# A decode block with an 8192-row KV cache: bias columns inside the first load, and the first load in 16 and 112 rows

## The chip, the cores and the metric

The kernel runs on one core of one Trainium2 chip. The metric is device time in microseconds (us) of one execution. Three executions of the kernel before took 1050.42, 1050.46 and 1050.50 us; the median is 1050.46 us. A profile of one more execution, of 1050.38 us, is what all views are taken from.

## The reference

One token goes through an attention block with a cached key and value store, and then through a dense block; both are modulated by a vector `c`. All data are float32. B_b1 and B_b2 are the two biases of the dense block; they are what the change handles differently.

```python
mod = (silu(c) @ w_mod).reshape(1, 6, 1, 640)          # sa, ca, ga, sb, cb, gb
h = layernorm(x) * (1 + ca) + sa
q = (h @ wq).reshape(32 heads, 192)
p = softmax(q . k_cache / sqrt(192))                   # 32 heads, 8192 keys each
o = p . v_cache                                        # 32 x 192
x = x + ga * (o @ wo)
h = layernorm(x) * (1 + cb) + sb
h = relu(h @ w1 + B_b1) ** 2                           # 640 -> 1536
x = x + gb * (h @ w2 + B_b2)                           # 1536 -> 640
```

The two caches are 32 x 8192 x 192 floats each, 403 MB together; the weights make up the rest of the 451.82 MB that the page of the profile counts as read.

## The kernel before

**Loads.** All loads go through one queue, issued by SyncE (SP in the profile) in the order of the program. The SBUF holds three large buffers, `slot`, of 128 rows, and every large load takes the next of the three in turn: first the load `first` (the modulation weights of two of the six parts, the query weights of the first pair of heads, and the columns of `c` and `x`, 8330 floats a row), then the keys of head 0, the values of head 0, the keys of head 1, and so on, `load_k(h)` and `load_v(h)`. Beside the keys, most rows of `in_kx` carry a piece of the weights `wq` or `wo` that a later step needs. Behind the last head come the weights of the dense block. A load into a slot waits until the work that read the slot's old content is done. So the keys of head 1 wait until all that reads `first` is done, the values of head 1 wait for the work on the keys of head 0, and the keys of head 2 for the work on the values of head 0. In this text k0 and v0 are the loads of keys and values of head 0, k1 and v1 those of head 1, and so on.

**Start.** Before head 0 can be worked on, the vector `silu(c)` is made (an exponential on ScalarE, ACT in the profile, then VectorE, DVE), the modulation of the first layer norm is weighed and summed (`weigh`, DVE and TensorE, PE), the layer norm is put together, and `query(0, ...)` multiplies its result with the query weights that lie in the slot of `first` (lines 352 to 381). Then `spread(x_c, KB, "x_t")` (line 382) copies the five columns of `x` on ACT to a tile `spread`, of which there is one buffer, each column 32 times side by side, and DVE transposes that to the tile `x_t`. This is the last read of the slot of `first`.

**A head.** `keys` multiplies the keys with the query in place (DVE, the group `slot<-slot,qb`), adds halves (GpSimd, POOL) and reduces (DVE, `sc`); `softmax` finds the maximum (DVE `mp`, PE transpose, DVE `nm`) and takes the exponential (ACT `p`); `values` multiplies with the values on PE. From head 1 on, `own` and `turn` bring the output of the head before into form.

**Biases.** The tile `bbc` holds 12 columns of B_b1 and 5 of B_b2. It is loaded after `load_v(0)` by four loads, of 8, 4, 12 and 104 rows of 17 floats (`BB_CUT`, lines 484 to 488). At head 3, before its `keys`, `spread(bbc, FB + KB, "bbt")` (line 490) brings them through the same tile `spread` to `bbt`, 544 floats a row. `bbt` is first read behind the last head, at lines 569 and 581.

**Waits.** A helper class records every operation and works out which semaphores it has to wait for; that is why nearly every row of the profile bears line 167. Each load counts on one of eight semaphores, `load0` to `load7`, in turn. Where an operation waits for several semaphores, the helper writes a wait for each, in front of the operation (lines 159 to 163):

```python
for w in waits:
    if w == "token":
        engine.wait_ge(sems[w], 1).then_inc(sems[w], -1)
    else:
        engine.wait_ge(sems[w[0]], w[1])
```

When the program is built, the last of these waits goes into the operation itself, and the others stay as instructions of their own ahead of it. The loads of ACT's function tables (`ACT_TABLE_LOAD`) are put in by the build, directly ahead of the operation that needs the table.

Of the kernel before, what the change touches and what calls it, by code (L numbers as in the profile page):

```python
# [11 lines left out]
P = 128  # L12
D = 640
# [7 lines left out]
KB = DG // 32  # L21
FB = FG // 32
# [5 lines left out]
WQ = KB * PW  # L28
ROW = KV + WO
WM = KB * 2 * D  # L30
VEC = 2 * KB
DA = 128
DB = DH - DA
REP = 8
# [2 lines left out]
WO_AT = {2 * i + 4: i for i in range(-1, NPAIR - 2)} | {H - 1: NPAIR - 2}  # L37
WQ_AT = {2 * i + 1: i + 1 for i in range(NPAIR - 1)}
WIDE = {h for h, i in (WO_AT | WQ_AT).items() if i >= 0}
BB_CUT = (8, 4, 12, 104)  # L40
HALF = DG // 2
W2_CUT = (0, 6 * D, 9 * D, 11 * D, 11 * D + G * HALF, FB * D)
EPS = 1e-5
# [180 lines left out]
    return b[1] <= a[1] and a[2] <= b[2] and b[3] <= a[3] and a[4] <= b[4]  # L224


def block_kernel(nc, first, kx, vx, wm1, w1, w2, bb, out):
    def const(shape, name):
        return nc.tile(shape, name)

    def work(shape, tag, bufs=2):
        return nc.tile(shape, tag, bufs)
# [6 lines left out]
    def slot():  # L239
        return nc.tile([P, ROW], "slot", 3, align=512)  # L240

    k_t, v_t = {}, {}
    first_t = slot()
    nc.sync.dma_start(first_t[:, :WM + WQ + VEC], first)

    ident = const([P, P], "ident")
    make_identity(nc, ident)
# [12 lines left out]
                            axis=AX.X, op=ALU.add)  # L260
# [3 lines left out]
                            axis=AX.X, op=ALU.add)  # L264
# [5 lines left out]

    vec = first_t[:, WM + WQ:WM + WQ + VEC]
    c_c = vec[:, :KB]
    x_c = vec[:, KB:2 * KB]
    bbc = const([P, FB + KB], "bbc")

    def load_k(h):
        k_t[h] = slot()
        n = K_PARTS.get(h, 1)
        cuts = [KV * c // n for c in range(n)] + [ROW if h in WIDE else KV]
        for a, b in zip(cuts, cuts[1:]):  # L280
            nc.sync.dma_start(k_t[h][:, a:b], kx[h, :, a:b])

    def load_v(h):
        v_t[h] = slot()
        nc.sync.dma_start(v_t[h][:, :KV], vx[h])
# [7 lines left out]
    def spread(src, n, name):  # L293

        t = work([P, FB + KB, 32], "spread", 1)
        nc.scalar.copy(t[:, :n], src[:, :, None].to_broadcast([P, n, 32]))
        r = const([P, 32 * n], name)
        nc.vector.transpose(r, t[:, :n].rearrange("p b r -> p (b r)"))
        return r

    def total(src, name):

        ps = psum("sm")
        n = src.shape[1]
        nc.tensor.matmul(ps[:, :n], ones, src, start=True, stop=True)
        return ps[:, :n]
# [35 lines left out]
    def attend(i, w, oT):  # L342

        nc.fresh = True
        for j in range(3):
            for g in range(G):
                nc.tensor.matmul(att[32 * g:32 * (g + 1), :DG], oT[:, j:j + 1].to_broadcast([P, 32]),
                                 w[:, j, DG * g:DG * (g + 1)], start=False, stop=(i == NPAIR - 1 and j == 2))
# [24 lines left out]
    def query(i, w):  # L373
        w = w.rearrange("p (b n) -> p b n", b=KB)
        ps = psum("q", at=0)
        for b in range(KB):
            nc.tensor.matmul(ps[:, :PW], h1[:, b:b + 1].to_broadcast([P, P]), w[:, b], start=(b == 0), stop=(b == KB - 1))
        qb_t[i] = work([P, PW], "qb")
        nc.scalar.activation(qb_t[i], ps[:, :PW], AF.Copy, scale=DH ** -0.5)

    query(0, first_t[:, WM:WM + WQ])
    x_t = spread(x_c, KB, "x_t")

    ri_t, o_t, sp_t, os_t, sum_t, m_t, pt_t = {}, {}, {}, {}, {}, {}, {}

    def keys(h, between):

        q = qb_t[h // 2][:, DH * (h % 2):DH * (h % 2 + 1)]
        sc = work([P, NPOS], "sc")
        t = k_t[h][:, :KV].rearrange("p (i d) -> p i d", d=DH)  # L390
        sums = SUMS.get(h, ((32, 0),))
        n = NPOS // len(sums)
        for c, (nf, na) in enumerate(sums):
            a, b = n - nf - na, n - na
            pr = t[:, c * n:(c + 1) * n]
            s = sc[:, c * n:(c + 1) * n]
            nc.vector.tensor_mul(pr, pr, q[:, None, :].to_broadcast([P, n, DH]))
            nc.gpsimd.tensor_add(pr[:, a:b, :DH // 2], pr[:, a:b, :DH // 2], pr[:, a:b, DH // 2:])
            for i in range(b, n):
                jk = work([P, DH], "jk")  # L400
                nc.scalar.activation(jk, pr[:, i], AF.Copy, accum_out=s[:, i:i + 1])
            nc.vector.tensor_reduce(s[:, :a], pr[:, :a], axis=AX.X, op=ALU.add)
            if c == 0:
                between()
            nc.vector.tensor_reduce(s[:, a:b], pr[:, a:b, :DH // 2], axis=AX.X, op=ALU.add)
        return sc

    def softmax(h, sc):
        mp = work([P, 1], "mp")
        nc.vector.tensor_reduce(mp, sc, axis=AX.X, op=ALU.max)  # L410
        ps = psum("sm")
        nc.tensor.transpose(ps[:, :P], mp.to_broadcast([P, P]), ident)
        nm = work([P, 1], "nm")
        nc.vector.tensor_reduce(nm, ps[:, :P], axis=AX.X, op=ALU.max, negate=True)

        p = work([P, NPOS, REP], "p", 1)
        i = h // 2
        if h % 2 == 0:
            sp_t[i] = work([P, 2], "sp", 3)
        nc.scalar.activation(p, sc[:, :, None].to_broadcast([P, NPOS, REP]), AF.Exp, bias=nm,  # L420
                             accum_out=sp_t[i][:, h % 2:h % 2 + 1])
        return p
# [17 lines left out]
    def own(h, after=None):  # L440

        i, a = h // 2, h % 2
        if not a:
            m_t[i] = work([P, 2, 1024], "own", 1)
            os_t[i] = work([P, P], "os", 3).rearrange("p (a d) -> p a d", a=2)
        if i not in ri_t and (a or i == NPAIR - 1):
            ri_t[i] = work([P, 2], "ri", 3)
            nc.vector.reciprocal(ri_t[i], sum_t.pop(i))
        m, o = m_t[i][:, a], o_t.pop(h)
        cuts = (0, 512, 1024) if h == H - 1 else (0, 1024)  # L450
        for lo, hi in zip(cuts, cuts[1:]):
            nc.vector.tensor_mul(m[:, lo:hi], o[:, lo:hi], mask[:, lo:hi], after=after)
        if i == NPAIR - 1:
            nc.vector.tensor_reduce(os_t[i][:, a], m[:, 512:].rearrange("p (j d) -> p d j", d=DB), axis=AX.X, op=ALU.add)
        elif a:
            nc.vector.tensor_reduce(os_t[i], m_t[i][:, :, 512:].rearrange("p a (j d) -> p a d j", d=DB), axis=AX.X, op=ALU.add)

    def turn(i, heads=(0, 1)):

        if i not in pt_t:  # L460
            pt_t[i] = psum("sm")
        pt = pt_t[i]
        for a in heads:
            nc.tensor.matmul(pt[DB * a:DB * (a + 1), 2:3], os_t[i][:, a], ri_t[i][:, a:a + 1], start=True, stop=True)
        for a in heads:
            for j in range(4):
                nc.tensor.matmul(pt[:, a:a + 1], m_t[i][:, a, DA * j:DA * (j + 1)], ri_t[i][:, a:a + 1],
                                 start=(j == 0), stop=(j == 3))
        if 1 in heads:
            oT_t[i] = work([P, 3], "oT", 3)  # L470
            nc.scalar.copy(oT_t[i], pt[:, :3])
# [4 lines left out]
    for h in range(H):  # L476
        i = h // 2
        if h % TURN == 1 and (h < H - 1 or nc.turns):
            nc.loop(h < H - 1)
        if h:  # L480
            load_k(h)
        load_v(h)
        if h == 0:
            nc.gpsimd.memset(v_t[0][:, KV:ROW], 0.0)
            r0 = 0
            for n in BB_CUT:
                nc.sync.dma_start(bbc[r0:r0 + n], bb[r0:r0 + n])
                r0 += n
        if h == 3:
            bbt = spread(bbc, FB + KB, "bbt")  # L490

        def wo():
            if h in WO_AT:
                attend(WO_AT[h], k_t[h][:, KV:ROW].rearrange("p (j n) -> p j n", j=3), oT_t.pop(WO_AT[h]))

        def between():
            if h in WQ_AT:
                query(WQ_AT[h], k_t[h][:, KV:ROW])
            if h < H - 1:
                wo()  # L500

        sc = keys(h, between)
        p = softmax(h, sc)
        if h == H - 1:
            sum_t[i] = total(sp_t.pop(i), f"sum{i}")
            wo()
        if h:
            own(h - 1, qb_t.get(h // 2 + 1))
        if h % 2 == 0 and h:
            turn(i - 1)  # L510
        if h == H - 1:
            turn(i, (0,))
        values(h, p)
        if h % 2 and h < H - 1:
            sum_t[i] = total(sp_t.pop(i), f"sum{i}")
# [132 lines left out]
```

## Time and profile before

| what | value |
|---|---|
| median of three runs | 1050.46 us (1050.42 to 1050.50) |
| time of the profiled execution | 1050.38 us |
| its span, first to last instruction | 1049.1 us |
| read from memory | 451.82 MB |
| instructions | 6398 |

Time and span differ by 1.3 us, which lie before the first and after the last instruction. In the views, times are microseconds from the start of the span. A row of the timeline reads: start, duration, engine (SPq is the queue of SyncE, PEld a weight load of PE), line, operation, destination<-sources, shape, count, and in brackets how long the engine had been idle and what ended that. A row of the windows reads: the stretch, its length, busy time of the five engines with their instruction counts, the granted TensorE clock, the share of the 16 DMA engines and the rate in GB/s. Packets are put into the window in which they start, whole, so in a short window share and rate can be far above what the engines can carry; they then tell how many packets started there.

### The profile page before, as it was taken

How to read it: one execution, taken by the hardware profiler on the slowest of the kernel's cores; microseconds unless marked ns; L12 is line 12 of the kernel's file. 1: busy time of each engine (PE TensorE's matmuls, PEld its weight loads, DVE VectorE, ACT ScalarE, POOL GpSimd, SP SyncE). 2: the span in 40 equal slices, each digit the busy share in tenths (PEclk: the TensorE clock that was granted, in tenths of full speed). 3: DMA queues.
4: the chain of work that ended last, by engine and by line, in shares of the span. 5: the costliest groups of instructions: out<-in, count | busy, mean ns of one | idle time of the engine just before them, and what ended most of it. 6: DMA issues, size and time to landing. Idle time of an engine off the chain costs nothing. (4 is left out here: it accounts for less than half of the span.)

```text
span 1049.1 us, 6398 instructions
## 1 busy us (share of the span) xinstructions
PE 457.0 (44%) x2736; PEld 207.5 (20%) x2736; DVE 829.3 (79%) x284; ACT 69.0 (7%) x247; POOL 213.3 (20%) x50
## 2 busy tenths in 40 slices
PE   1153452535445064453526355163443516353456
PEld 0011221112122031222203122121212103121223
DVE  6788778988787987878888787897878798778852
ACT  1000000000000000000000000000000000012330
POOL 1221122221122221022222022222012222022100
PEclk9666665766657576675666658566665766666569
DMA  9999999999999999999999999999999999999998
GB/s 403 446 429 430 419 448 433 422 448 431 430 427 437 445 424 440 435 435 429 428 446 431 431 426 444 437 427 437 437 430 427 435 444 433 428 440 435 428 424 357
DMA packets 11266, 451.99 MB, mean 431 GB/s; under 512 B 1525, under 2 KB 1781, under 8 KB 2037
## 3 DMA queue, kind: packets, MB, share of 16 engines
q1 hardware_dynamic: 11253, 451.83, 99.6%
q8 instruction: 7, 0.11, 0.0%
q14 instruction: 6, 0.05, 0.0%
HBM read 451.82 MB, written 0.00 MB: 431 GB/s over the span
## 5 line engine op out<-in xcount | busy, mean ns | idle before, releaser
L167 DVE TENSOR_TENSOR slot<-slot,qb 128x12288 f32<-128x12288 f32 (+2 forms) x37 | 415.3, 11225 | 133.3 <-DMA slot<-in_kx 133.3
L167 POOL TENSOR_TENSOR slot<-slot 128x3072 f32<-128x3072 f32 (+2 forms) x37 | 210.3, 5683 | 791.6 <-DVE slot L167 791.6
L167 DVE TENSOR_REDUCE sc<-slot 128x32 f32<-128x6144 f32 (+5 forms) x74 | 307.0, 4150 | 13.3 <-POOL slot L167 12.0
L167 PE MATMUL ps_o<-slot,p 128*32 128x512 f32 x1536 | 240.8, 791 | 22.2 <-PEq L161 21.0
L167 PE MATMUL ps_q<-slot,ln_h 128*128 128x384 f32 x160 | 88.9, 728 | 80.6 <-PEq L161 79.3
L167 PE MATMUL ps_sm<-ident,mp 128*128 128x128 f32 x32 | 14.0, 438 | 248.9 <-PEq L161 213.0
L167 PEld LDWEIGHTS ps_o<-slot,p 128*32 128x32 f32 x1536 | 63.4, 140 | 175.3 <-issue 171.6
L167 PE MATMUL ps_q<-slot,oT 128*32 128x160 f32 x408 | 29.5, 453 | 154.6 <-PEq L161 154.4
L167 PEld LDWEIGHTS ps_q<-slot,ln_h 128*128 128x128 f32 x160 | 45.4, 296 | 128.5 <-issue 122.7
L167 PEld LDWEIGHTS ps_sm<-ident,mp 128*128 128x128 f32 x32 | 5.7, 179 | 267.3 <-issue 229.9
L167 ACT ACTIVATE p<-sc,nm 128x512 f32<-128x512 f32 x32 | 23.1, 721 | 525.7 <-DVE nm L167 525.7
L167 PE MATMUL ps_sm<-ri,own 128*128 128x1 f32 x256 | 56.5, 350 | 0.0
L167 PEld LDWEIGHTS ps_sm<-ri,own 128*128 128x128 f32 x256 | 55.0, 326 | 0.2
L167 PEld LDWEIGHTS ps_q<-slot,oT 128*32 128x32 f32 x408 | 18.2, 158 | 158.1 <-issue 155.2
L167 DVE TENSOR_TENSOR own<-ps_o,mask 128x1024 f32<-128x1024 f32 (+1 forms) x33 | 38.9, 1178 | 9.5 <-PE ps_o L167 9.5
L167 DVE TENSOR_REDUCE os<-own 128x128 f32<-128x1024 f32 (+1 forms) x17 | 30.2, 1774 | 0.6
L167 PE MATMUL ps_sm<-ri,os 128*64 128x1 f32 x64 | 6.4, 247 | 55.1 <-POOLq L165 54.4
L167 DVE TENSOR_REDUCE nm<-ps_sm 128x1 f32<-128x128 f32 x32 | 9.3, 292 | 21.2 <-PE ps_sm L167 21.2
L167 ACT ACTIVATE jk<-slot 128x192 f32<-128x192 f32 x69 | 24.0, 349 | 32.0 <-DVE slot L167 32.0
L167 ACT ACTIVATE qb<-ps_q 128x384 f32<-128x384 f32 x16 | 7.8, 490 | 272.8 <-PE ps_q L167 272.8
L167 PEld LDWEIGHTS ps_sm<-ri,os 128*64 128x64 f32 x64 | 5.3, 203 | 60.4 <-issue 58.4
L167 ACT ACTIVATION_READ_ACCUMULATOR jk<-slot 128x1 f32 x69 | 12.9, 187 | 0.0
(81 smaller groups left out, 93.4 us busy)
## 6 DMA issues: line engine op xcount, KB each, us to landing
slot<-in_kx SPq DMA_DIRECT2D x28, 7104.0 KB, 28.1
slot<-in_vx SPq DMA_DIRECT2D x32, 6144.0 KB, 22.6
slot<-in_kx SPq DMA_DIRECT2D x2, 6144.0 KB, 25.4
slot<-in_kx SPq DMA_DIRECT2D x2, 4032.0 KB, 23.8
slot<-in_kx SPq DMA_DIRECT2D x2, 3072.0 KB, 16.9
slot<-in_first SPq DMA_DIRECT2D x1, 4165.0 KB, 12.5
slot<-in_wm SPq DMA_DIRECT2D x1, 3840.0 KB, 25.5
slot<-in_w SPq DMA_DIRECT2D x1, 3840.0 KB, 31.8
```

Source lines behind the costliest of these rows:

```text
L167: i = getattr(engine, name)(*args, **kwargs)
```

## The change

The 17 bias columns become part of the rows of `first`: the host appends them, so that a row has 8347 floats, and `bbc` is now a view of the slot. The four bias loads and `BB_CUT` go. `first` is loaded by two loads, rows 0 to 15 and rows 16 to 127, instead of one. `spread(bbc, FB + KB, "bbt")` moves from head 3 to directly behind the one of `x_t`, because the slot is overwritten by k1.

```diff
-VEC = 2 * KB
+VEC = 3 * KB + FB
-BB_CUT = (8, 4, 12, 104)
...
     first_t = slot()
-    nc.sync.dma_start(first_t[:, :WM + WQ + VEC], first)
+    for a, b in ((0, 16), (16, P)):
+        nc.sync.dma_start(first_t[a:b, :WM + WQ + VEC], first[a:b])
...
-    bbc = const([P, FB + KB], "bbc")
+    bbc = vec[:, 2 * KB:]
...
     query(0, first_t[:, WM:WM + WQ])
     x_t = spread(x_c, KB, "x_t")
+    bbt = spread(bbc, FB + KB, "bbt")
...
         if h == 0:
             nc.gpsimd.memset(v_t[0][:, KV:ROW], 0.0)
-            r0 = 0
-            for n in BB_CUT:
-                nc.sync.dma_start(bbc[r0:r0 + n], bb[r0:r0 + n])
-                r0 += n
-        if h == 3:
-            bbt = spread(bbc, FB + KB, "bbt")
...
-        "first": np.concatenate([rows(wm[:, :2 * D], KB), wq[0], column(c, KB), column(a(A_x).ravel()[order], KB)], axis=1),
+        "first": np.concatenate([rows(wm[:, :2 * D], KB), wq[0], column(c, KB), column(a(A_x).ravel()[order], KB),
+                                 column(B_b1, FB), column(a(B_b2)[order], KB)], axis=1),
```

Two places show what the built programs have in another order. The first is ACT at the start, up to the exponential of the first head. In brackets stand the semaphores that are waited for ahead of a row or by it; `load0` and `load1` are those of the first and the second load of the program. Before:

```order
L167 ACT_TABLE_LOAD [waits barrier_Pool_Activation_PE_DVE_SP_release]
L167 ACTIVATE silu<-slot 128x5 [waits load0]
L167 ACT_TABLE_LOAD
L167 ACTIVATE ln_sd<-ps_sm,eps_t 128x1 [waits tensor]
L167 ACTIVATE qb<-ps_q 128x384 [waits tensor]
L167 COPY spread<-slot 128x160
L167 ACT_TABLE_LOAD
L167 ACTIVATE p,sp<-sc,nm 128x512 [waits vector]
```

The same place of ACT in the changed program:

```order
L166 ACT_TABLE_LOAD [waits barrier_Pool_Activation_PE_DVE_SP_release,load1]
L166 ACTIVATE silu<-slot 128x5 [waits load0]
L166 ACT_TABLE_LOAD
L166 ACTIVATE ln_sd<-ps_sm,eps_t 128x1 [waits tensor]
L166 ACTIVATE qb<-ps_q 128x384 [waits tensor]
L166 COPY spread<-slot 128x160
L166 COPY spread<-slot 128x544 [waits vector]
L166 ACT_TABLE_LOAD
L166 ACTIVATE p,sp<-sc,nm 128x512 [waits vector]
```

Two things moved: the exponential now depends on two loads, and the wait for the second of them (`load1`, the 112 rows) stands ahead of the first table load; and the copy of the bias columns stands behind the copy for `x_t`, with a wait for DVE.

The second place is DVE around the first head, from the transpose to `x_t` to the multiplication of the second head's keys. Before:

```order
L167 STREAM_TRANSPOSE x_t<-spread 128x160 [waits scalar]
L167 TENSOR_TENSOR slot<-slot,qb 128x12288 [waits load1]
L167 TENSOR_REDUCE sc<-slot 128x32 [waits vector]
L167 TENSOR_REDUCE sc<-slot 128x32 [waits gpsimd]
L167 TENSOR_REDUCE mp<-sc 128x1 [waits vector]
L167 TENSOR_REDUCE nm<-ps_sm 128x1 [waits tensor]
L167 TENSOR_TENSOR slot<-slot,qb 128x12288 [waits load7]
```

The same place of DVE in the changed program:

```order
L166 STREAM_TRANSPOSE x_t<-spread 128x160 [waits scalar]
L166 STREAM_TRANSPOSE bbt<-spread 128x544 [waits scalar]
L166 TENSOR_TENSOR slot<-slot,qb 128x12288 [waits load2]
L166 TENSOR_REDUCE sc<-slot 128x32 [waits vector]
L166 TENSOR_REDUCE sc<-slot 128x32 [waits gpsimd]
L166 TENSOR_REDUCE mp<-sc 128x1 [waits vector]
L166 TENSOR_REDUCE nm<-ps_sm 128x1 [waits tensor]
L166 TENSOR_TENSOR slot<-slot,qb 128x12288 [waits load4]
```

The transpose to `bbt` now stands ahead of the first large multiplication; before, it stood ahead of that of head 3.

More of the change, by code (lines that the diff above doesn't have):

```diff
@@ L224, in within, with block_kernel @@
     return b[1] <= a[1] and a[2] <= b[2] and b[3] <= a[3] and a[4] <= b[4]
-def block_kernel(nc, first, kx, vx, wm1, w1, w2, bb, out):
+def block_kernel(nc, first, kx, vx, wm1, w1, w2, out):
     def const(shape, name):
@@ L637 @@
         "w2": w2,
-        "bb": np.concatenate([column(B_b1, FB), column(a(B_b2)[order], KB)], axis=1),
     }
```

## The prediction

> **What bounds the kernel now.** I read the page of the profile first, then the chain that ended last, then windows over the whole span. The page says how full the memory path is.
>
> ```profile
> span 1049.1 us, 6398 instructions
> PE 457.0 (44%) x2736; PEld 207.5 (20%) x2736; DVE 829.3 (79%) x284; ACT 69.0 (7%) x247; POOL 213.3 (20%) x50
> q1 hardware_dynamic: 11253, 451.83, 99.6%
> ...
> 1.50:5.00 3.50, 0.00 (x0) 0.00 (x0) 2.92 (x1) 0.51 (x1) 2.31 (x7) 1.00 1.00 343
> 102.00:1020.00 918.00, 406.46 (x2311) 184.94 (x2306) 742.44 (x227) 60.54 (x230) 196.02 (x35) 0.64 1.00 433
> ...
> 1020.41 25.14 DMA slot<-in_w
> 1045.55 0.04 issue
> 1045.59 1.17 PE ps_q L167 x32
> ```
>
> The reader is to see that the packets of queue q1 fill 99.6% of the span of 16 DMA engines, that the share is 1.00 at 433 GB/s in the long middle, and that the chain ends in the last weights (`in_w`) with two microseconds of work behind them. DVE, the busiest engine, has 79%. So the time is the start of the stream of loads, plus 452 MB at the rate of the middle, plus a short end, plus every stretch in which the stream has no load to work on. The end is not edited. The change can act by an earlier or later start of the stream, by bytes and packets, and by a gap. The queue has a gap when SP issues a load too late, and SP issues a load when its slot is free. So I looked for how early each load is issued. These rows are from the timeline (the queue of SP and what holds it at the start) and from the lists of DMA issues (number, KB, time from issue to landing).
>
> ```profile
> 0.73 1.28 ACT L167 ACT_TABLE_LOAD   x1 [0.73 <-PEq L640]
> 0.74 0.38 SPq L167 DMA_DIRECT2D slot<-in_first  x1
> 1.18 0.42 SPq L167 DMA_DIRECT2D slot<-in_kx  x1
> 2.11 1.77 SPq L167 DMA_DIRECT2D bbc<-in_bb  x4
> 13.30 0.21 ACT L167 ACTIVATE silu<-slot 128x5 f32<-128x5 f32 x1 [11.29 <-DMA slot<-in_first]
> 30.90 0.32 ACT L167 COPY spread<-slot 128x160 f32<-128x160 f32 x1
> 31.24 0.36 SPq L167 DMA_DIRECT2D slot<-in_kx  x1
> 31.25 0.35 DVE L167 STREAM_TRANSPOSE x_t<-spread 128x160 f32<-128x160 f32 x1 [6.82 <-ACT spread L167]
> 31.51 12.92 DVE L167 TENSOR_TENSOR slot<-slot,qb 128x12288 f32<-128x12288 f32 x1
> 54.61 0.35 SPq L167 DMA_DIRECT2D slot<-in_vx  x1
> 59.11 12.96 DVE L167 TENSOR_TENSOR slot<-slot,qb 128x12288 f32<-128x12288 f32 x1 [3.42 <-DMA slot<-in_kx]
> ...
> slot<-in_first SPq DMA_DIRECT2D x1, 4165.0 KB, 12.5
> slot<-in_kx SPq DMA_DIRECT2D x1, 7104.0 KB, 27.9
> slot<-in_vx SPq DMA_DIRECT2D x1, 6144.0 KB, 18.9
> ...
> slot<-in_kx SPq DMA_DIRECT2D x1, 6144.0 KB, 24.2
> slot<-in_vx SPq DMA_DIRECT2D x1, 6144.0 KB, 21.8
> ```
>
> The five rows of issues are, in order, `first` (0.74), k1 (31.24), v1 (54.61), k2 and v2 (both issued between 63 and 83). `first` is the only large load that met an empty queue. Its 4165 KB are 4.27 MB, 9.8 us at 433 GB/s; it took 12.5. So a load on an empty queue costs 2.7 us beside its bytes. What another load takes beyond its bytes and these 2.7 us is time that it stood in line, and by so much it could be issued later without a gap:
>
> - k1: 7.27 MB are 16.8 us; 27.9 - 16.8 - 2.7 = 8.4 us.
> - v1: 6.29 MB are 14.5 us; 18.9 - 14.5 - 2.7 = **1.7 us**.
> - k2: 24.2 - 14.5 - 2.7 = 7.0 us. v2: 21.8 - 14.5 - 2.7 = 4.6 us.
>
> The load of the values of head 1 has the least slack at the start, 1.7 us, and it waits for DVE to be done with head 0, which in turn hangs on the prologue. A second look at the same place: packets that start around the change from k1 to v1.
>
> ```profile
> 1.70:2.00 0.30, 0.00 (x0) 0.00 (x0) 0.00 (x0) 0.30 (x1) 0.24 (x2) 1.00 5.27 1333
> 2.60:2.75 0.15, 0.00 (x0) 0.00 (x0) 0.15 (x1) 0.00 (x0) 0.15 (x1) 1.00 2.36 889
> 41.25:42.05 0.80, 0.00 (x0) 0.00 (x0) 0.80 (x1) 0.00 (x0) 0.00 (x0) 0.50 2.78 1148
> 57.90:58.15 0.25, 0.25 (x4) 0.00 (x0) 0.00 (x0) 0.00 (x0) 0.00 (x0) 0.50 0.00 0
> 58.15:58.80 0.65, 0.65 (x8) 0.20 (x4) 0.00 (x0) 0.00 (x0) 0.00 (x0) 0.50 2.81 1210
> ```
>
> All 16 engines begin v1 between 58.15 and 58.80: 1210 GB/s over 0.65 us are 0.79 MB, sixteen rows of 49 KB. At the very start 1333 GB/s over 0.30 us are twelve rows of 33 KB from 1.70 on, and four follow after 2.60. Issue was at 0.74, so a packet starts about 1.0 us after its issue, on four engines 1.9 us. For v1, issued at 54.61, that is 55.6 on most engines and 56.5 on four: 2.5 us, or 1.6 us, ahead of 58.15, when the first engine comes free. The two ways to see the slack, 1.7 us and about 2.5 us, differ by the slower first packets of a cold queue.
>
> **The change, part by part.**
>
> *Bytes.* The 8.7 KB of biases are loaded either way: 0.
>
> *Four small loads out of the queue.* SP spent 1.77 us on them at 2.11 and had nothing to issue until 31.24, so nobody gains that. Their packets lie between v0 and k1: there the sixteen engines change loads within 0.80 us (1148 GB/s are sixteen rows of 57 KB), while the change to v1 takes 0.65. So their worth is 0 to 0.15 us at that place; I take 0.1. But k1 then also ends 0.1 us earlier, and the slack of v1 is smaller by as much, so it counts only where no gap opens.
>
> *First load in two.* It moves the start of the stream. Bounds: a gain of 0.9 us if the four late engines start with the others and all of that lasts to the landing; a loss of 0.45 us if the rows of the second load, issued one place later (1.18 instead of 0.74), are missed. On the first engines a row of 33 KB lasts over 1.2 us (33,320 bytes at 433/16 GB/s), which covers the 0.45; so a loss is less near than a gain, and a gain on the first packets is partly lost in the cold start. I take a gain of 0.1 us, range -0.3 (loss) to +0.4. [...]
>
> *A table load behind the wait.* Before, the table load ran at 0.73 while `first` was on its way, and the exponential started at 13.30, when it landed. In the changed order the wait for `load1`, the 112 rows that land last, stands ahead of the table load. So from the landing on, 1.28 us pass before the exponential, and everything up to the query of head 0 is later by that. What follows the table load directly on ACT can be read at the end of the kernel:
>
> ```profile
> 1008.99 1.28 ACT L167 ACT_TABLE_LOAD   x1
> 1010.28 0.20 ACT L167 ACTIVATE warm<-eps_t 128x1 f32<-128x1 f32 x1
> ```
>
> There an operation starts 1.29 us after the table load started. So I take 1.28. [...]
>
> *The bias spread ahead of head 0.* Its prices stand at head 3 now:
>
> ```profile
> 119.77 0.64 ACT L167 COPY spread<-bbc 128x544 f32<-128x544 f32 x1
> 120.45 0.74 DVE L167 STREAM_TRANSPOSE bbt<-spread 128x544 f32<-128x544 f32 x1 [4.93 <-ACT spread L167]
> 121.12 12.92 DVE L167 TENSOR_TENSOR slot<-slot,qb 128x12288 f32<-128x12288 f32 x1
> ```
>
> The tile `spread` has one buffer, so the copy on ACT waits until DVE has read it for `x_t`: 31.25 + 0.35 = 31.60. Then 0.64 for the copy, 0.04 to the transpose (119.77 + 0.64 = 120.41, start 120.45), and 0.67 from its start to the next operation (121.12 - 120.45): 32.95, with 0.02 for the first handover 32.97. The multiplication of head 0 started at 31.51, so it is 1.46 us later. Queued behind the waiting transpose on DVE is all of head 0. On ACT the copy is followed by the table load at 31.23, which has until 55.7 and costs nothing. SP's issue of k1 moves from 31.24 by 1.28 + 1.0, and k1 has 8.4 us: nothing.
>
> *Head 3 without it.* DVE waited there for ACT's copy until 120.45. What is late next is the landing of k3 itself. Since the stream of loads sets the pace, the DVE time that comes free is worth 0.
>
> *Sum.* v1 is issued 1.28 + 1.46 = 2.74 us later against the landing of `first`, with 1.7 us of slack. By the slack the stream stands still for 2.74 - 1.7 = 1.0 us. By the packets' start it does less: 54.61 + 2.74 + 1.0 = 58.35, when some engines have been free for 0.2 us and others are busy until 58.80, and only the cold start of the packets is paid in part. So the gap is 0 to 1.0 us; I take 0.7, nearer to the end that the one empty-queue load showed. It goes through to the end, since the stream never rests later. DVE itself has 3.42 us of waiting ahead of head 1 (59.11), more than 2.74, so head 1 isn't later through DVE. The 2.74 us eat into no other load: k2 waits for PE on v0, which is later by the same 2.74, and has 7.0; v2 hangs on the landing of k1 and not on head 0.
>
> Gap +0.7, first load -0.1: +0.6 us. The profiled execution took 1050.38 us (span 1049.1 and 1.3 around it) and becomes 1051.0; the median of the runs lies 0.08 higher, so the forecast is **1051.1 us**. A measurement of this kernel can tell about 0.2%, 2.1 us; the forecast is inside that.
>
> **The rivals.**
>
> *No gap.* Should v1's descriptors reach the engines while their last rows of k1 still run, as the packets' start nearly allows, the cover holds. It holds for certain if the table load doesn't come behind the wait after all (delay 1.46, slack 1.7). Then only the gains are left: 0.1 for the small loads and 0.1 for the first load, up to 0.4: 1050.46 - 0.2 = 1050.3 us, down to 1050.0. For it: 58.35 is ahead of the last engines. Against: the order of the changed program shows the wait ahead of the table load.
>
> [...]
>
> *An earlier start.* If starting with 16 rows brings all engines to work 0.9 us earlier and no gap opens, the time is 1050.46 - 0.9 - 0.1 = 1049.5 us, still within 0.2%. Nothing in the sum reaches a gain of 2.1 us.
>
> **How the numbers follow.** Forecast with a gap of some tenths to a microsecond (1050.5 to 1051.9): 0.64. No gap (1050.0 to 1050.4): 0.26. Wide gap (1052.8): 0.05. Large gain at the start (1049.5): 0.05. The range of 1050.0 to 1051.9 us takes the first two: the lower end is no gap and the full 0.4 of the first load, the upper a gap of 1.0 and a loss of 0.3 at the first load with 0.1 for the rest. Of the chances, the forecast, "no gap" and most of the large gain are within 0.2%: 0.93; slower 0.05; faster 0.02, for an error of over a microsecond in the case of the earlier start.
>
> **What would show it.** In the changed profile: the first table load of ACT at about 13.2 and not at 0.7, the exponential at 14.5; the transpose to `bbt` next to that of `x_t`, and head 0's multiplication at about 34.2; v1 issued at about 57.3, landing in 17 us and not 18.9; no packet start at 58.2 where v1's stood. DVE's wait ahead of head 1 shrinks from 3.42 us to under 1. If v1's first packets still start by 58.8 the gap was none; if the exponential starts over 2 us after the landing, the table load is dearer than its row.

## The result, and the profile after

The changed kernel takes 1061.45 us in the median of five runs (1061.24 to 1062.79); the kernel before took 1050.44 us beside it (1050.39 to 1050.50). The ratio is 1.0109, with a 95% interval of 1.0094 to 1.0124: 11 us slower, where 0.6 us was forecast and 1051.9 us was the upper end of the range.

The page of the changed kernel, from an execution of 1062.64 us, shows where to look first.

```profile
span 1061.2 us, 6391 instructions
DMA  9999999999999999999999999999999999999998
GB/s 250 450 408 425 443 424 441 431 428 439 422 434 434 441 430 426 438 435 433 434 436 432 428 437 437 435 434 430 441 422 439 433 436 434 430 440 426 439 423 338
q1 hardware_dynamic: 11104, 451.83, 99.5%
```

The row of GB/s of the kernel before:

```profile
GB/s 403 446 429 430 419 448 433 422 448 431 430 427 437 445 424 440 435 435 429 428 446 431 431 426 444 437 427 437 437 430 427 435 444 433 428 440 435 428 424 357
```

The DMA engines are as busy as before, 99.5% (99.6% before). But in the first slice of 26.5 us they move 250 GB/s instead of 403; the other slices, the last one aside, lie between 408 and 450, before between 419 and 448. A busy DMA engine isn't a fast one: the row of tenths hides this, the row of GB/s tells it. The next rows are windows of the changed kernel: one that takes in all 128 rows of `first`, one in which only rows of the second load start, two short ones in which one round of sixteen rows starts, and stretches behind `first`.

```profile
1.50:20.60 19.10, 0.76 (x8) 0.23 (x8) 7.09 (x2) 0.00 (x0) 2.31 (x7) 1.00 1.00 224
1.70:2.30 0.60, 0.00 (x0) 0.00 (x0) 0.22 (x1) 0.00 (x0) 0.55 (x6) 1.00 6.15 890
2.50:20.50 18.00, 0.76 (x8) 0.23 (x8) 6.67 (x2) 0.00 (x0) 1.46 (x1) 1.00 0.86 208
8.10:8.70 0.60, 0.00 (x0) 0.00 (x0) 0.60 (x1) 0.00 (x0) 0.00 (x0) 1.00 3.82 890
22.00:66.00 44.00, 7.38 (x22) 3.79 (x22) 33.10 (x24) 5.66 (x8) 6.68 (x1) 0.76 1.00 433
67.00:69.60 2.60, 1.73 (x11) 0.42 (x15) 1.13 (x1) 0.81 (x2) 0.00 (x0) 0.50 0.97 321
118.00:1020.00 902.00, 393.15 (x2226) 178.65 (x2226) 736.71 (x223) 57.63 (x225) 193.45 (x35) 0.65 1.00 433
```

The same 18 us of the kernel before, in which `first` ends and the keys of head 0 begin:

```profile
2.50:20.50 18.00, 1.91 (x12) 1.24 (x12) 13.43 (x16) 1.75 (x3) 1.46 (x1) 1.00 1.00 433
```

While `first` is loaded the engines move 224 GB/s, or 208 where the sixteen rows of the first load, which start ahead of 2.50, are left out. In each short window 890 GB/s over 0.60 us are sixteen rows of 33 KB; share times length is how long each lasts, 6.15 x 0.60 = 3.7 us in the first load and 3.82 x 0.60 = 2.3 us at 8.10. From the keys of head 0 on it is 433, with a dip to 321 at about 67, where v1 follows k1, and then 433 again. So the loss lies at two places near the start. The issues (`first`, then v1) and the timeline of the changed kernel show the same from the side of the engines.

```profile
slot<-in_first SPq DMA_DIRECT2D x1, 3651.8 KB, 21.6
slot<-in_first SPq DMA_DIRECT2D x1, 521.7 KB, 6.6
...
slot<-in_vx SPq DMA_DIRECT2D x1, 6144.0 KB, 19.6
...
0.74 0.85 SPq L166 DMA_DIRECT2D slot<-in_first  x2
22.87 1.28 ACT L166 ACT_TABLE_LOAD   x1 [22.87 <-DMA slot<-in_first]
24.17 0.21 ACT L166 ACTIVATE silu<-slot 128x5 f32<-128x5 f32 x1
41.44 0.64 ACT L166 COPY spread<-slot 128x544 f32<-128x544 f32 x1 [0.41 <-DVE x_t L166]
42.11 0.33 SPq L166 DMA_DIRECT2D slot<-in_kx  x1
42.12 0.74 DVE L166 STREAM_TRANSPOSE bbt<-spread 128x544 f32<-128x544 f32 x1 [0.71 <-ACT spread L166]
42.78 12.92 DVE L166 TENSOR_TENSOR slot<-slot,qb 128x12288 f32<-128x12288 f32 x1
65.89 0.33 SPq L166 DMA_DIRECT2D slot<-in_vx  x1
68.47 12.96 DVE L166 TENSOR_TENSOR slot<-slot,qb 128x12288 f32<-128x12288 f32 x1 [1.50 <-DMA slot<-in_kx]
```

`first` lands at 22.87 and not at 13.30: 9.6 us later. The table load stands behind that landing and the bias copy and transpose ahead of head 0, both as the order had shown. Of the 12.3 us between the two profiled executions, 9.6 are there before the first operation that reads `first`. The multiplication of head 1, which waits for k1, is later by 68.47 - 59.11 = 9.4 us. v1 lands at 65.89 + 19.6 = 85.5, in the kernel before at 54.61 + 18.9 = 73.5: 12.0 us later. So the remaining 2.6 us are lost between the landings of k1 and v1.

### The profile page after: what moved, and what is told of

Same layout as the page of the kernel before. It is cut to its first block, busy times and chain, and to the rows that moved or that the text cites. A ratio compares the mean times of both kernels' runs of the same rounds, so it can differ in the third digit from the quotient of the medians.

```text
span 1061.2 us, 6391 instructions
## 1 busy us (share of the span) xinstructions
PE 455.6 (43%) x2736; PEld 206.5 (19%) x2736; DVE 829.4 (78%) x284; ACT 69.0 (7%) x247; POOL 213.3 (20%) x50
## 3 DMA queue, kind: packets, MB, share of 16 engines
q1 hardware_dynamic: 11104, 451.83, 99.5%
## 5 line engine op out<-in xcount | busy, mean ns | idle before, releaser
L166 PE MATMUL ps_q<-slot,ln_h 128*128 128x384 f32 x160 | 86.6, 712 | 76.7 <-PEq L160 75.4
```

The source lines that it names most:

```text
L166: i = getattr(engine, name)(*args, **kwargs)
```

## The experiments

The first theory was that the new length of the rows, 33,388 bytes, an odd number of floats, slows each packet. The rivals were the split by rows, and the delay of head 0. The first four kernels tell these apart. Kernels timed together share the runs of the kernel before, 1050.43 us for these four.

**One float more in each row.** The edit:

```diff
-VEC = 3 * KB + FB
+VEC = 3 * KB + FB + 1
...
```

> The changed kernel with one float of zeros more at the end of each row of first (8348 floats, 33,392 bytes); all else as changed. Theory 'row shape' (the row of 33,388 bytes is what made the packets of first take 2.28 us in place of 1.24): first lands at about 13 us again, its packets take about 1.25 us, and the time falls back from 1061.4 us to 1050.4 to 1051.9 us, as the prediction had it, with a gap at the values of head 1 of 0 to 1 us. Theory 'split' (the load in 16 and 112 rows spreads badly over the engines): first still lands at about 22 us and the time stays at about 1061 us. Theory 'wait and bias spread' (the delay of head 0 costs the 11 us): about 1061 us too, but with first landing early.

Measured: 1061.21 us (1060.12 to 1061.93), ratio 1.0100 (1.0084 to 1.0117); `first` lands at 23.08. An even number of floats doesn't help; the load by 128 rows below settles the theory of the row shape.

**One load of 128 rows.** The edit:

```diff
-    for a, b in ((0, 16), (16, P)):
-        nc.sync.dma_start(first_t[a:b, :WM + WQ + VEC], first[a:b])
+    nc.sync.dma_start(first_t[:, :WM + WQ + VEC], first)
```

> The changed kernel with first loaded by one load of 128 rows of 8347 floats. Theory 'row shape': still slow, first lands at 20 to 23 us, about 1060 us. Theory 'split': first lands at about 13 us, 1050 to 1052 us. With one load the table load stands ahead of the wait again, so the exponential starts right at the landing.

Measured: 1051.38 us in one run, and the exponential at 13.60. With rows of the same odd length the 9.6 us are gone.

**The split alone.** The kernel before, with the loop over 16 and 112 rows of 8330 floats and nothing else.

> The kernel before with only the split into 16 and 112 rows (rows of 8330 floats; the four bias loads and the spread at head 3 stay). Theory 'row shape': 1050.1 to 1051 us, first lands at about 13 us, the first table load of ScalarE stands behind that landing. Theory 'split': about 1059 to 1061 us, first lands at about 22 us.

Measured: 1060.30 us (1059.87 to 1061.28), ratio 1.0096 (1.0080 to 1.0113). So the split by rows, with the rows of before, brings 9.9 of the 11.0 us. The issues and the timeline of this kernel:

```profile
slot<-in_first SPq DMA_DIRECT2D x1, 3644.4 KB, 21.5
...
22.77 1.28 ACT L167 ACT_TABLE_LOAD   x1 [22.77 <-DMA slot<-in_first]
64.47 0.35 SPq L167 DMA_DIRECT2D slot<-in_vx  x1
```

**Rows that start at multiples of 128 bytes.** The tensor is padded to 8352 floats a row, of which 8347 are loaded in 16 and 112 rows.

> The changed kernel with the rows of first 8352 floats (33,408 bytes) apart in memory, of which the same 8347 are loaded. So each row starts at a multiple of 128 bytes of the tensor but is still 33,388 bytes long. If the length is what is slow: first lands at about 22 us, about 1061 us. If the start addresses (only every second row started at a multiple of 8 bytes) are what is slow: first lands at about 13 us, 1050 to 1052 us.

Measured: 1063.18 us in one run, `first` at 22.99. Neither length nor start address matters.

That left the question what it is about the split: that there are two loads, that one is small, where in memory they read, or where in the SBUF they write. The next four kernels were made for that; the kernel before took 1050.41 us beside them.

**A split by columns.** Two loads again, each of 128 rows:

```diff
-    for a, b in ((0, 16), (16, P)):
-        nc.sync.dma_start(first_t[a:b, :WM + WQ + VEC], first[a:b])
+    cut = WM // 2
+    for a, b in ((0, cut), (cut, WM + WQ + VEC)):
+        nc.sync.dma_start(first_t[:, a:b], first[:, a:b])
```

> The changed kernel with first split by columns: two loads, each of all 128 rows, the first with the front half of the modulation weights. Theory 'rows' (what is slow is a load that covers few rows, because the engines then write into the same part of the SBUF): first lands at about 13 us, 1050.4 to 1051.9 us. Theory 'two loads' (any second load ahead of the stream costs): first lands at about 22 us, about 1061 us.

Measured: 1051.10 us (1050.22 to 1052.02), ratio 1.0006 (0.9996 to 1.0016); the second load lands 12.0 us after its issue. Two loads by themselves cost nothing that can be measured.

**Rows in two halves.** `((0, 64), (64, P))` in place of `((0, 16), (16, P))`.

> The changed kernel with first in rows 0 to 63 and 64 to 127. [...] Theory 'small first load' (16 rows of one row per engine are what is bad): first lands at 13 to 15 us, 1051 to 1053 us.

Measured: 1062.07 us in one run, `first` at 23.91. A small first load isn't what is bad either.

**Eight loads of 16 neighbouring rows, and eight loads of every eighth row.** Both read the same 16 neighbouring rows of memory in each load; only the rows of the SBUF differ.

```diff
-LANES = 8
+LANES = 16
...
-    for a, b in ((0, 16), (16, P)):
+    for a, b in [(16 * j, 16 * j + 16) for j in range(8)]:
         nc.sync.dma_start(first_t[a:b, :WM + WQ + VEC], first[a:b])
```

```diff
...
-    for a, b in ((0, 16), (16, P)):
-        nc.sync.dma_start(first_t[a:b, :WM + WQ + VEC], first[a:b])
+    for j in range(8):
+        nc.sync.dma_start(first_t[j:P:8, :WM + WQ + VEC], first[16 * j:16 * j + 16], apart=True)
...
+    arrays["first"] = np.ascontiguousarray(arrays["first"].reshape(16, 8, -1).transpose(1, 0, 2).reshape(P, -1))
```

`LANES` is the number of load semaphores, 16 in both kernels. `apart` tells the helper that these loads need not wait for one another. The last line permutes the rows in memory, so that each lands where it belongs.

> The changed kernel with first in eight loads of 16 neighbouring rows (16 load semaphores instead of 8, so that the keys of head 0 don't wait for the first of them). [...] Theory 'number of loads' or 'memory side': the same as the next kernel, which reads the same rows of memory in the same loads.

> As the kernel with eight loads of 16 rows, with the same 16 neighbouring rows of memory in each load, but written to every eighth row of the SBUF (rows 0, 8, 16 ... then 1, 9, 17 ...; the rows are permuted in memory so that each lands where it belongs). [...] Theory 'memory side' or 'number of loads': no difference between the two.

Measured, one run each: 1078.49 us with neighbouring rows, 1062.37 us with every eighth. The rates while `first` was loaded stand in windows of the four kernels; first the one with a split by columns:

```profile
2.50:12.00 9.50, 0.76 (x8) 0.23 (x8) 6.68 (x2) 0.00 (x0) 1.46 (x1) 1.00 1.00 423
```

The one with halves of 64 rows:

```profile
2.50:21.50 19.00, 0.76 (x8) 0.23 (x8) 6.68 (x2) 0.00 (x0) 1.46 (x1) 1.00 0.98 204
```

The one with 16 neighbouring rows in a load:

```profile
2.50:37.50 35.00, 0.76 (x8) 0.23 (x8) 6.69 (x2) 0.00 (x0) 1.46 (x1) 1.00 0.94 111
...
39.56 1.28 ACT L166 ACT_TABLE_LOAD   x1 [39.56 <-DMA slot<-in_first]
```

The one with every eighth row:

```profile
2.50:21.50 19.00, 0.76 (x8) 0.23 (x8) 6.69 (x2) 0.00 (x0) 1.47 (x1) 1.00 0.96 199
...
23.73 1.28 ACT L168 ACT_TABLE_LOAD   x1 [23.73 <-DMA slot<-in_first]
```

Nearly the same share of busy engines, 0.94 to 1.00, moves 423, 204, 111 and 199 GB/s. The last two read the same memory in the same number of loads and differ in the rows of the SBUF that each load writes: 16 neighbouring ones moved at 111 GB/s, 16 that lie eight apart at 199. So the rows of the SBUF that a load writes count here, and neither where in memory it reads nor the number of loads explains the two rates. Loads of neighbouring rows ran the faster the more rows they wrote, 111 with 16 and 204 with 64, and the two loads of the split by columns, which write all 128, ran at 423. The load of 112 rows, seven eighths of the data here, doesn't fit into that order: it ran at 208, no faster than those of 64. The profiles show these rates; what in the SBUF sets them isn't shown by any run here.

The last four kernels take up what the forecast was about, the delay of head 0. The kernel before took 1050.45 us beside them.

**One load, in eleven runs.** The kernel with one load of 128 rows, as above.

> The changed kernel with first as one load of 128 rows, timed closely. Head 0 is late by the bias spread alone (1.46 us). Theory 'slack' of the prediction (the values of head 1 can be issued 1.7 us later at no cost): 1050.3 to 1050.5 us, no loss. Theory 'cold start is paid earlier' (the first packets of that load already slow down when it is issued less than about 2 us ahead of the end of the load before): 0.5 to 1.0 us slower than before, as in the single look.

Measured: 1051.80 us (1050.32 to 1053.51), ratio 1.0012 (1.0003 to 1.0021).

**One load, and the bias spread at head 3 again.** On top of the one load:

```diff
-    bbt = spread(bbc, FB + KB, "bbt")
+    bbk = const([P, FB + KB], "bbk")
+    nc.scalar.copy(bbk, bbc)
...
+        if h == 3:
+            bbt = spread(bbk, FB + KB, "bbt")
```

> As the kernel with one load of 128 rows, but the 17 bias columns are copied on ScalarE to a small tile of their own, and the spread stands at head 3 again. Head 0 is no longer late. Both theories: the gap at the values of head 1 is gone, their first packets take 1.82 us, and the time is that of before or at most 0.3 us below it (the four small loads are gone): 1050.1 to 1050.5 us.

Measured: 1050.42 us (1050.28 to 1050.90), ratio 1.0000 (0.9991 to 1.0009). It has the biases in the rows of `first` and no bias loads, and is as fast as the kernel before, not faster.

**A split by columns that the exponential waits for.** `cut = WM + WQ + 2` in the split by columns: the cut lies within the columns of `c`.

> The changed kernel with first in two loads of all 128 rows, cut by columns within the columns of c, so that the exponential waits for both loads and the first table load stands behind the landing. Head 0 is late by 1.28 + 1.46 = 2.74 us, as the prediction had it, but the loads cover all rows. Theory 'slack': gap of 1.0 us at most, 0.7 taken, 1051.0 to 1051.4 us. Theory 'cold start is paid earlier': 1.3 to 2.2 us slower than before, 1051.8 to 1052.6 us.

Measured: 1052.19 us (1051.19 to 1052.70), ratio 1.0016 (1.0007 to 1.0025).

**The same, with the bias spread at head 3.**

> As the kernel cut within the columns of c, but with the bias spread at head 3. Head 0 is late by the table load alone, 1.28 us. Theory 'slack': no loss, 1050.2 to 1050.6 us. Theory 'cold start is paid earlier': 0.3 to 0.8 us slower than before.

Measured: 1051.01 us (1050.80 to 1051.98), ratio 1.0005 (0.9996 to 1.0014).

How late v1 is issued, and what becomes of its sixteen first packets, shows in the timeline and in the window in which these packets start. With the spread at head 3 and one load:

```profile
53.70 0.33 SPq L166 DMA_DIRECT2D slot<-in_vx  x1
...
57.95:58.80 0.85, 0.85 (x12) 0.23 (x8) 0.00 (x0) 0.00 (x0) 0.00 (x0) 0.74 2.15 925
```

With the table load behind the landing and the spread at head 3:

```profile
56.77 0.33 SPq L166 DMA_DIRECT2D slot<-in_vx  x1
...
58.10:59.06 0.96, 0.30 (x4) 0.20 (x8) 0.00 (x0) 0.61 (x2) 0.00 (x0) 0.50 2.27 819
```

With the table load behind the landing and the spread ahead of head 0:

```profile
57.68 0.33 SPq L166 DMA_DIRECT2D slot<-in_vx  x1
...
58.60:59.25 0.65, 0.00 (x0) 0.00 (x0) 0.17 (x2) 0.45 (x1) 0.00 (x0) 0.50 4.07 1210
```

The rate says that sixteen packets of 49 KB start in each window (925 x 0.85, 819 x 0.96 and 1210 x 0.65 are 0.79 MB). Share times length is how long one of them lasts: 1.83, 2.18 and 2.65 us; in the kernel before it was 2.81 x 0.65 = 1.83. So in these profiles the later v1 is issued, the more its first packets drag, up to 0.8 us, and in the last kernel they also start 0.4 us later than the 58.15 of before.

## Why the prediction was wrong

**First load in two: the step that failed.** The prediction bounded it by where the engines start and by the issue of the second load: "On the first engines a row of 33 KB lasts over 1.2 us (33,320 bytes at 433/16 GB/s), which covers the 0.45". It took for granted that 16 rows or 112 move at the rate of 128; instead such a row lasted 3.7 us in the first load and 2.3 us at 8.10 in the second. No row of the profile of before says so: the only loads there with fewer than 128 rows are the tiny ones of the biases. So the trace of before set no upper bound for this price, and the range left that out. The term of 0.1 us of gain measured 9.9 us of loss, in the kernel with the split alone. With 64 and 64 rows the load ran at 204 GB/s, about half of the 423 with the split by columns.

**Bytes** were right. **The four small loads** were worth nothing that can be measured (ratio 1.0000 without them, in the kernel with the spread at head 3), as against the 0.1 us allowed.

**The table load behind the wait** is where the order had it, and costs 24.17 - 22.87 = 1.30 us on ACT: the exponential starts 0.02 us after the load's 1.28.

**The bias spread ahead of head 0** was priced well. The ten matmuls of the query stand just ahead of it; their rows, after and before:

```profile
35.35 4.94 PE L166 MATMUL ps_q<-slot,ln_h 128*128 128x384 f32 x10 [1.30 <-DVE ln_h L166]
```

```profile
24.48 5.99 PE L167 MATMUL ps_q<-slot,ln_h 128*128 128x384 f32 x10 [1.31 <-DVE ln_h L167]
```

From their end to the multiplication of head 0 it is 42.78 - 40.29 = 2.49 us in the changed kernel and 31.51 - 30.47 = 1.04 us in the kernel before: 1.45 us more, forecast 1.46. What the forecast didn't have is that these matmuls themselves don't always take as long: 4.94 and 5.99 us in the two rows, at a granted clock of 1.00 both times. With the split by columns they took about 6.51, an estimate from ACT's idle time ahead of `qb`, which they end: 11.31 us there and 10.79 in the kernel before, and 5.99 + 11.31 - 10.79 = 6.51. From the exponential to head 0 the changed kernel is therefore only 18.61 - 18.21 = 0.40 us later than before. With one load it is 19.60 us, 1.39 later. These are the rows of the first profile with one load:

```profile
13.60 0.21 ACT L166 ACTIVATE silu<-slot 128x5 f32<-128x5 f32 x1 [11.59 <-DMA slot<-in_first]
33.20 12.92 DVE L166 TENSOR_TENSOR slot<-slot,qb 128x12288 f32<-128x12288 f32 x1
56.30 0.33 SPq L166 DMA_DIRECT2D slot<-in_vx  x1
```

**The gap at v1** was the right place, but too small a size. The kernel that has the delays of the forecast, but loads all rows together, takes 1.74 us more than before; the forecast had a gap of 0 to 1.0 and took 0.7. By the time of its issue, 57.68 - 54.61 = 3.07 us late, the slack of 1.7 would give 1.4. For the table load alone it is 56.77 - 54.61 - 1.7 = 0.46, measured 0.56, an interval that holds zero. One load of 128 rows, in eleven runs, lost 1.35 us, more than that way of counting gives for its issue at 56.66 (0.35). In the changed kernel v1 is issued 68.47 - 65.89 = 2.58 us ahead of head 1, before 59.11 - 54.61 = 4.50; that is 1.9 us later, of which a slack of 1.7 would leave 0.2, and 2.6 were lost in its profile. So the slack was read too large. The theory that the cold start is paid earlier does better in the last four expectations: its range holds for two of its three losses, and the loss of one load, 1.35, lies above its 0.5 to 1.0. But the time of the issue alone doesn't set the loss: with v1 issued at 56.66 the median lost 1.35 us, with 56.77 only 0.56 (the two profiled runs 1.64 and 0.82). What else does, and what makes the runs with one load scatter by 3 us, is open; the changing length of the query's matmuls moves the issue of v1 and is a candidate that no run here isolates.

**Wide gap, no gap, earlier start:** none of the three came. The 1052.8 us of the wide gap stood on a table load that costs more than its row, which no run shows: from its start to the exponential it is 1.30 us in the changed kernel, and 1.29 or 1.30 in every other profile where it stands behind the landing. The slower side came true through the split by rows, 9.9 of the 11.0 us, and the loss at v1 in the changed kernel's profile, 2.6 us, came without a dearer table load.

## What to carry to other kernels

Where a load like this one has to be split, split it by columns and not by rows: all 128 rows by part of the columns ran at 423 GB/s, 64 rows at 204, 16 and 112 rows at 208 to 224, 16 neighbouring rows at 111, and the engines were about equally busy each time. When a profile holds no load of the shape that a change brings in, its rate is unknown, and the range must say so. And when an operation comes to wait for two loads, look where the second wait lands: here it pulled a table load of 1.3 us behind the landing.

## What was not expected of the hardware

The busy share of the DMA engines reads 0.86 to 1.00 at anything from 111 to 433 GB/s: a packet that takes longer, 2.3 us at 8.10 for a row that was reckoned at 1.2, counts as busy for all of it.

A load that is issued shortly before the engines come to it drags, even where its packets start no later than before. At an issue of 56.77 the first packets of v1 last 2.18 us in place of 1.83, although they start from 58.10 on, as early as those of the kernel before (58.15). In these profiles the limit lies between 1.3 us, from that issue to that start, and 2.2 us: in the kernel with the split alone, issued at 64.47 and starting 2.2 us later, they last 1.52 x 1.20 = 1.82 us as before:

```profile
66.70:67.90 1.20, 1.20 (x8) 0.20 (x4) 0.00 (x0) 0.00 (x0) 0.00 (x0) 0.50 1.52 655
```
